# Which engine normalises the attention rows in the first slots, and where the second sum of a weight conversion stands on Pool

## The chip, the cores and the metric

The kernel runs on one core of one Trainium2 chip. The metric is the device time of one execution in microseconds (us). The engines are named as the profile names them: PE (matrix products and transposes), DVE (vector), ACT (activations and most copies), POOL or Pool (GpSimd), SP (which here only issues transfers, DMAs). Each engine runs its own queue of instructions in order and waits on semaphores for the others.

## What is computed

```python
B, H, S, D = 8, 8, 576, 64;  top_k = 32          # q, k, v: (B, H, S, D)
scores = (q @ k.T) / sqrt(D)
kth    = 32nd largest score of each row
scores = where(scores >= kth, scores, -1e9)
attn   = exp(scores - rowmax);  attn = attn / (sum(attn) + 1e-9)
x      = (attn @ v) as (B*S, H*D) = (4608, 512)
out    = gelu_exact(x @ w_in) @ w_out             # w_in (512, 2048), w_out (2048, 512)
```

q, k and v are float32; w_in and w_out arrive as float64 and are converted in the kernel.

## The kernel before

**Items and slots.** The attention is cut into 144 items. An item is 128 rows of scores for a pair of heads side by side (the last 64 rows of four heads are packed into one item), in one tile `s` of 128 partitions x 2 x 576. The loop at L616 makes one pass per item, plus four; I call a pass a slot, n counts them from 0. The order of the work is written out by hand: there is no scheduler, each engine gets its instructions in the order in which the loop emits them. Several items are in work at once. Slot n does, in this order:

- `weights_add` of the weight unit that belongs to slot n (L619; see below), the scores of item n + 2 (L620, PE into PSUM, and ACT copies them to `s`, L280 and L281), the product with v of item n - 3 (L621, PE L443, every second slot, then an ACT copy to `xT`, L448);
- transposes of item n - 2 (L624): first the tails (PE L394, ACT copy L395), then four each of the two halves (PE L412, ACT copies L419). Their PSUM buffers are two, shared with other small products, so the second half waits until ACT has emptied the tails' buffer;
- the softmax of item n - 1 on ACT (L362 masks with the threshold `neg`, L363 is the exponential with the row's sum into `den`), for both halves before the tails' copy up to slot 10, and for one half before and one behind it later (`late`, L622);
- `add_small` of item n - 1 on Pool (L355: `den` + 1e-9);
- `top_k` of item n on DVE (L323 and L326: four rounds of the eight largest for two halves), with `inverse` (L349: 1 / `den` of item n - 1, into `rden`) at its end;
- `threshold` of item n on Pool (L338 and L341: `neg` and `bias`, which the softmax of item n needs in slot n + 1);
- `normalise` of item n - 1 (L375, s times `rden`, one instruction per half): on Pool, on DVE, or one half each, by its second argument (L660);
- `weights_size` of the unit of slot n + 1 on ACT (L174, L176 and, before slot 10, L178), and the loads on SP: `load_weights` of the unit of slot n + 2 (L664, L159), and `v` (L666).

Between these the loop places pieces of the two MLP products (`mlp`, PE L495 and L531, ACT's GELU L506), as soon as there are finished rows of `xT`: the first stands in slot 10.

**The weights.** The two weight matrices come in 16 units of 128 x 1024 numbers. A unit of float64 words is loaded into a staging area, and is turned into float32 by whole-number arithmetic: ACT makes two or three parts from the words (`weights_size`), and Pool adds them up: `weights_add` does the first sum (L193) and the second (L194). Units stand in slots 1 to 15 and 17. From slot START = 10 on (`on_pool`) one of ACT's parts is made by Pool instead (L190). The staging area of a unit is loaded again for the unit two slots later, so that load waits for the second sum.

**Who normalises before.** Where slot n + 1 has a weight unit of START or later, DVE normalises both halves; where it has an earlier one, Pool has the first half and DVE the second; where it has none, Pool has both.

Of the kernel before, what the change touches and what calls it, by code (L numbers as in the profile page):

```python
# [14 lines left out]
def kernel(  # L15
# [97 lines left out]
    def weights_of(u):  # L113

        if u < NWI:
            c, r = u // 2 * WS, u % 2 * 2
            return w_in, r, c, w_in_sb[:, r : r + 2, c : c + WS]
        r = 2 * (u - NWI)
        return w_out, r, 0, w_out_sb[:, r : r + 2, :]
# [6 lines left out]
    words = {}  # L126
# [8 lines left out]
    unit_in = UNIT_IN.get  # L135
# [29 lines left out]
    def parts(u):  # L165

        t, dst = words[u], weights_of(u)[3].bitcast(i32)
        return t[:, :, 0::2], t.bitcast(mybir.dt.int16)[:, :, 2::4], t[:, :, 1::2].bitcast(i32), dst
# [11 lines left out]
    def on_pool(u):  # L180

        return SLOT_OF[u] >= START

    made = set()

    def weights_add(u):
        if u in words:
            w, _, below, d = parts(u)
            if on_pool(u):
                nc.gpsimd.tensor_scalar(  # L190
                    w.bitcast(i32), w.bitcast(u32), 2.0**-13, None, op0=ALU.mult
                )
            nc.gpsimd.tensor_tensor(d, d, below, op=ALU.add)  # L193
            nc.gpsimd.tensor_tensor(d, d, w.bitcast(i32), op=ALU.add)  # L194
        made.add(u)


    items, starts = [], []
# [47 lines left out]
    def row(i, e):  # L246
        return S_of[i][:, e * S : (e + 1) * S]
# [60 lines left out]
    def top_k(i, hooks):  # L308


        stat_of[i] = st = {
            "top": work.tile([P, 2, TOPK], f32, tag="top", name="top"),
            "neg": work.tile([P, 2, 2], f32, tag="neg", name="neg"),
            "bias": work.tile([P, 2], f32, tag="bias", name="bias"),
            "den": work.tile([P, 2], f32, tag="den", name="den"),
            "rden": work.tile([P, 2], f32, tag="rden", name="rden"),
        }
        cur = [row(i, e) for e in range(2)]
        rest = work.tile([P, 2, S], f32, tag="rest", bufs=1, name="rest")
        n_op = 0  # L320
        for r in range(TOPK // 8):
            for e in range(2):
                nc.vector.max(st["top"][:, e, 8 * r : 8 * r + 8], cur[e])  # L323
            if r < TOPK // 8 - 1:
                for e in range(2):
                    nc.vector.match_replace(  # L326
                        rest[:, e], st["top"][:, e, 8 * r : 8 * r + 8], cur[e], LOWEST
                    )
                cur = [rest[:, e] for e in range(2)]
            if r in hooks:  # L330
                hooks.pop(r)()

    def threshold(i):

        if i < 0 or i >= N:
            return
        st = stat_of[i]
        nc.gpsimd.tensor_scalar(  # L338
            st["neg"], st["top"][:, :, 0 :: TOPK - 1], -1.0, None, op0=ALU.mult
        )  # L340
        nc.gpsimd.tensor_tensor(  # L341
            st["bias"], st["neg"][:, :, 0], st["neg"][:, :, 1], op=ALU.subtract
        )

    def inverse(i):
        if i < 0 or i >= N:
            return
        st = stat_of[i]
        nc.vector.reciprocal(st["rden"], st["den"])  # L349

    def add_small(i):
        if i < 0 or i >= N:
            return
        st = stat_of[i]
        nc.gpsimd.tensor_scalar(st["den"], st["den"], 1e-9, None, op0=ALU.add)  # L355

    def softmax(i, e):

        if i < 0 or i >= N:
            return  # L360
        st, s = stat_of[i], row(i, e)
        nc.scalar.activation(s, s, func=AF.Prelu, bias=st["neg"][:, e, 1:2], scale=1.0, alpha=STEEP)  # L362
        nc.scalar.activation(  # L363
            s, s, func=AF.Exp, bias=st["bias"][:, e : e + 1], scale=1.0,
            accum_out=st["den"][:, e : e + 1],
        )

    def normalise(i, on_dve):

        if i < 0 or i >= N:  # L370
            return
        st = stat_of[i]
        for e in range(2):
            s = row(i, e)
            (nc.vector if e >= 2 - on_dve else nc.gpsimd).tensor_scalar(  # L375
                s, s, st["rden"][:, e : e + 1], None, op0=ALU.mult
            )
# [5 lines left out]
    def transposes(i):  # L383

        if i < 0 or i >= N:
            return []
        t, s = items[i][1], S_of.pop(i)

        def tails():
            tp = ps.tile([P, 512], f32, tag="tp", name="tp_t")  # L390
            if t < NM:
                if t % 2 == 0:
                    pt_now[0] = work.tile([P, 2 * NM + 1, 2 * P], f32, tag="pt", name="pt")
                nc.tensor.transpose(tp[:, 0:P], s[:, SM : S + TL], ident)  # L394
                nc.scalar.copy(out=pt_now[0][:, 2 * NM, t % 2 * P : (t % 2 + 1) * P], in_=tp[:, 0:P])  # L395
            else:
                pt_now[0] = ptt
                for r in range(2):
                    nc.tensor.transpose(
                        tp[0:TL, r * P : (r + 1) * P], s[:, r * S + SM : (r + 1) * S], ident  # L400
                    )
                for e in range(2):
                    c = slice(e * TL, (e + 1) * TL)
                    nc.scalar.copy(
                        out=halves(ptt[c, 0, NM, :], e, NJ * P), in_=halves(tp[0:TL, 0 : 2 * P], e, P)
                    )

        def main(e):
            tp = ps.tile([P, 512], f32, tag="tp", name="tp")
            first = e * (S + TL if t < NM else S)  # L410
            for j in range(NM):
                nc.tensor.transpose(  # L412
                    tp[:, j * P : (j + 1) * P], s[:, first + j * P : first + (j + 1) * P], ident
                )
            if t < NM:
                dst = pt_now[0][:, e * NM : (e + 1) * NM, t % 2 * P : (t % 2 + 1) * P]
            else:
                dst = ptt[:, e, 0:NM, :]
            nc.scalar.copy(out=dst, in_=tp.rearrange("p (j n) -> p j n", j=NM))  # L419

        return [tails] + [lambda e=e: main(e) for e in range(2)]
# [137 lines left out]
    def run_gelus():  # L559
        while waiting:  # L560
            gelus(waiting.pop(0))
# [9 lines left out]
    def mlp(n):  # L571
        for _ in range(n):
            if done[0] >= len(pieces) or pieces[done[0]][0] > ready[0] or left[0] == 0:
                return
            pieces[done[0]][1]()
            done[0] += 1
            left[0] -= 1
# [38 lines left out]
    for n in range(ahead):  # L616

        left[0] = 7 if START < n < START + 2 * NP else 8
        weights_add(unit_in(n))  # L619
        scores(n + 2)  # L620
        product = attend(n - 3)  # L621
        late = n > START  # L622
        mlp(1)
        tr = transposes(n - 2)  # L624
        if product and n > START and done[0] < len(pieces) and pieces[done[0]][0] > ready[0]:

            for piece in tr[:1]:
                piece()
            tr, ready[0] = tr[1:], n_tok[0]
        softmax(n - 1, 0)  # L630
        mlp(1)
        if not late:
            softmax(n - 1, 1)
        mlp(1)
        prep = prep_in.pop(n, [])
        if len(prep) > 1 and len(tr) == 3:
            tr, prep = tr[:1] + prep[:1] + tr[1:], prep[1:]
        for piece in tr[:-1]:
            piece()
            ready[0] = n_tok[0]  # L640
            mlp(1)
        ready[0] = n_tok[0]
        if late:
            softmax(n - 1, 1)
        add_small(n - 1)
        for piece in tr[-1:] + prep:
            piece()
            mlp(1)

        run_gelus()  # L650
        mlp(left[0])
        run_gelus()
        if n < N:
            top_k(n, {3: lambda: inverse(n - 1)})
        else:
            inverse(n - 1)
        threshold(n)
        u = unit_in(n + 1)

        normalise(n - 1, 0 if u not in words else 2 if on_pool(u) else 1)  # L660

        weights_size(unit_in(n + 1))
        if n >= FIRST:
            load_weights(n + 2)  # L664
        if n <= NP:
            load("v", n)  # L666
# [38 lines left out]
```

## Time and profile before

| | |
|---|---|
| time, three runs | median 1655.15 us (1654.75 to 1656.08) |
| the profiled execution | 1655.42 us, its span 1653.7 us |
| busy in the span: PE, DVE, ACT, Pool | 1593.8, 1419.6, 1184.1, 650.5 us |
| normalising on Pool (L375) | 266 instructions, 1723 ns each |
| normalising on DVE (L375) | 22 instructions, 520 ns each (median) |
| second sums on Pool (L194) | 16 instructions, about 2.40 us each |
| busy on Pool between 33.0 and 43.3 us (about slot 2) | 7.23 of 10.3 us |
| busy on DVE in the same stretch | 10.27 of 10.3 us |
| first product of the MLP on PE (L495) | starts at 117.94 us |

Times inside an execution count from the start of its span. A row of the timeline gives the start, the duration, the engine, the line, the operation and its tiles; in brackets stands how long the engine had been idle before it and what released it. A row of the waits gives who waited for whom: total us, how often, and the longest. A row of the chain that ended last gives start, duration, engine, tile and line of each step, followed back from the last instruction. The granted clock is PE's, 1.0 at full speed.

### The profile page before, as it was taken

How to read it: one execution, taken by the hardware profiler on the slowest of the kernel's cores; microseconds unless marked ns; L12 is line 12 of the kernel's file. 1: busy time of each engine (PE TensorE's matmuls, PEld its weight loads, DVE VectorE, ACT ScalarE, POOL GpSimd, SP SyncE). 2: the span in 40 equal slices, each digit the busy share in tenths (PEclk: the TensorE clock that was granted, in tenths of full speed). 3: DMA queues.
4: the chain of work that ended last, by engine and by line, in shares of the span. 5: the costliest groups of instructions: out<-in, count | busy, mean ns of one | idle time of the engine just before them, and what ended most of it. 6: DMA issues, size and time to landing. Idle time of an engine off the chain costs nothing.

```text
span 1653.7 us, 25056 instructions
## 1 busy us (share of the span) xinstructions
PE 1593.8 (96%) x8832; PEld 1080.5 (65%) x8832; DVE 1419.6 (86%) x3049; ACT 1184.1 (72%) x2131; POOL 650.5 (39%) x756
## 2 busy tenths in 40 slices
PE   6669999999999999999999999999999999999999
PEld 4346566766666667676666667676666666666665
DVE  7999899989999889998989988998889898999800
ACT  6888777777777777777777777777777777777720
POOL 3677543333333333333333333333333333333300
PEclk7669999999999999999999999999999999999999
DMA  6423210011101111011110111001110001000000
GB/s 165 139 98 102 83 43 1 14 29 29 50 1 28 30 30 28 1 28 36 29 28 1 42 29 43 1 14 28 44 35 1 27 15 34 2 14 4 4 13 13
DMA packets 126621, 56.14 MB, mean 34 GB/s; under 512 B 117760, under 2 KB 117792, under 8 KB 126496
## 3 DMA queue, kind: packets, MB, share of 16 engines
q1 hardware_dynamic: 125376, 54.25, 12.2%
q8 instruction: 70, 1.15, 0.3%
q14 instruction: 55, 0.45, 0.1%
q10 hardware_dynamic: 1056, 0.26, 0.1%
q0 software_dynamic: 64, 0.03, 0.0%
HBM read 45.08 MB, written 9.44 MB: 33 GB/s over the span
## 4 chain that ended last, share of the span: by engine, by line
PE 92%; ACT 6%; DVE 1%; issue 1%; POOL 0%; ACTq 0%; POOLq 0%; DVEq 0%
PE h_ps L495 30%; PE y_ps L531 30%; PE o L443 9%; PE s_ps L276 8%; PE tp L412 8%; PE tp_qk L231 2%; PE t_ps L272 2%; ACT s L363 1%; PE o L454 1%; ACT s L362 1%; PE s_ps L297 1%; PE tp_t L394 1%; ACT s L280 1%; POOL s L375 0%; PE warm L595 0%
## 5 line engine op out<-in xcount | busy, mean ns | idle before, releaser
L323 DVE MAX8 top<-rest 128x8 f32<-128x576 f32 x864 | 608.9, 746 | 0.0
L495 PE MATMUL h_ps<-xT,w_in_sb 128*128 128x256 f32 (+1 forms) x2560 | 554.5, 362 | 3.8 <-ACT g L506 3.8
L531 PE MATMUL y_ps<-w_out_sb,g 128*128 128x512 f32 x1152 | 549.5, 599 | 0.0
L495 PEld LDWEIGHTS h_ps<-xT,w_in_sb 128*128 128x128 f32 x2560 | 429.6, 191 | 66.6 <-issue 19.6
L375 POOL TENSOR_SCALAR s<-s,rden 128x576 f32<-128x576 f32 x266 | 456.0, 1723 | 0.8 <-issue 0.4
L326 DVE MATCH_REPLACE8 rest<-top,rest 128x576 f32<-128x576 f32 x576 | 423.0, 741 | 0.0
L355 POOL TENSOR_SCALAR den<-den 128x2 f32<-128x2 f32 x144 | 32.0, 222 | 835.2 <-ACT s L363 834.4
L531 PEld LDWEIGHTS y_ps<-w_out_sb,g 128*128 128x128 f32 x1152 | 195.1, 190 | 166.8 <-issue 165.0
L280 ACT ACTIVATE s<-s_ps 128x1024 f32<-128x1024 f32 x128 | 131.5, 1027 | 167.3 <-PE s_ps L276 149.1
L363 ACT ACTIVATE s<-s,bias 128x576 f32<-128x576 f32 x288 | 223.3, 776 | 13.3 <-ACT s L362 0.7
L362 ACT ACTIVATE s<-s,neg 128x576 f32<-128x576 f32 x288 | 223.9, 778 | 0.3 <-POOL neg L338 0.2
L419 ACT COPY pt<-tp 128x512 f32<-128x512 f32 x256 | 147.1, 574 | 103.0 <-PE tp L412 103.0
L412 PEld LDWEIGHTS tp<-ident,s 128*128 128x128 f32 x1152 | 145.9, 144 | 111.9 <-issue 59.1
L326 DVE MATCH_REPLACE8 rest<-top,s 128x576 f32<-128x576 f32 x288 | 211.6, 742 | 0.0
L323 DVE MAX8 top<-s 128x8 f32<-128x576 f32 x288 | 201.8, 742 | 3.9 <-ACT s L281 3.9
L412 PE MATMUL tp<-ident,s 128*128 128x128 f32 x1152 | 178.6, 279 | 23.6 <-ACT pt L395 22.0
L443 PE MATMUL o<-pt,raw_v 128*64 128x256 f32 x1280 | 155.5, 390 | 0.0
L276 PE MATMUL s_ps<-qk 64*128 64x256 f32 x1024 | 153.9, 421 | 0.7 <-ACT s L280 0.7
L349 DVE RECIPROCAL rden<-den 128x2 f32<-128x2 f32 x144 | 23.0, 160 | 142.1 <-POOL den L355 141.8
L443 PEld LDWEIGHTS o<-pt,raw_v 128*64 128x64 f32 x1280 | 87.8, 139 | 66.2 <-issue 23.4
L276 PEld LDWEIGHTS s_ps<-qk 64*128 64x128 f32 x1024 | 92.5, 195 | 23.7 <-issue 1.6
L506 ACT ACTIVATE g<-h_ps 128x512 f32<-128x512 f32 x144 | 78.6, 595 | 34.0 <-PE h_ps L495 33.2
(66 smaller groups left out, 1088.3 us busy)
## 6 DMA issues: line engine op xcount, KB each, us to landing
raw_q<-in_q_dram SPq DMA_DIRECT2D x64, 128.0 KB, 2.4
raw_v<-in_v_dram SPq DMA_DIRECT2D x64, 128.0 KB, 2.5
out_dram<-y SPq DMA_DIRECT2D x32, 256.0 KB, 2.1
w_out_sb<-in_moe_w_in_dram SPq DMA_DIRECT2D x16, 511.8 KB, 4.9
raw_k<-in_k_dram SPq DMA_DIRECT2D x62, 128.0 KB, 2.5
w_out_sb<-in_moe_w_out_dram SPq DMA_DIRECT2D x10, 511.8 KB, 3.9
words<-in_moe_w_out_dram SPq DMA_DIRECT2D x6, 511.8 KB, 4.5
raw_q<-in_q_dram SPq DMA_DIRECT2D x64, 16.0 KB, 2.3
```

The costliest lines, as they stand in the source:

```text
L276: nc.tensor.matmul(s_ps[:, e, c * 256 : (c + 1) * 256], lhsT=lhsT[rows, :], rhs=qk[rows, KT + c * 256 : KT + (c + 1) * 256], start=True, s ...
L280: nc.scalar.activation(spread(s, S + TL, SM), s_ps, func=AF.Copy, scale=scale)
L323: nc.vector.max(st["top"][:, e, 8 * r : 8 * r + 8], cur[e])
L326: nc.vector.match_replace(rest[:, e], st["top"][:, e, 8 * r : 8 * r + 8], cur[e], LOWEST)
L362: nc.scalar.activation(s, s, func=AF.Prelu, bias=st["neg"][:, e, 1:2], scale=1.0, alpha=STEEP)
L363: nc.scalar.activation(s, s, func=AF.Exp, bias=st["bias"][:, e : e + 1], scale=1.0, accum_out=st["den"][:, e : e + 1],)
L375: (nc.vector if e >= 2 - on_dve else nc.gpsimd).tensor_scalar(s, s, st["rden"][:, e : e + 1], None, op0=ALU.mult)
L412: nc.tensor.transpose(tp[:, j * P : (j + 1) * P], s[:, first + j * P : first + (j + 1) * P], ident)
L419: nc.scalar.copy(out=dst, in_=tp.rearrange("p (j n) -> p j n", j=NM))
L443: nc.tensor.matmul(o[e * D : (e + 1) * D, 0:n], lhsT=vt[:, j, e, :], rhs=pt[:, e * NM + j if j < NM else 2 * NM, :], start=(j == 0), stop= ...
L495: nc.tensor.matmul(h_tile(u)[:, i, :], lhsT=w_in_sb[:, ko, f * P : (f + 1) * P], rhs=xT[:, ko, c0 : c0 + n], start=(ko == 0), stop=(ko == ...
L531: nc.tensor.matmul(y_of[sub], lhsT=g_of[u][:, i, sub * P : (sub + 1) * P], rhs=w_out_sb[:, f, :], start=(f == 0), stop=(f == FT - 1),)
```

## The change

In the first slots (weight units of slots 2 to 9) DVE normalises nothing any more, Pool does both halves. From START on it is as before. The second sum of each weight unit goes into a function of its own, `weights_end`, which is called behind `add_small`, in all 16 slots that have a unit; the first sum and, from START on, L190 stay at the start of the slot.

```diff
                 nc.gpsimd.tensor_tensor(d, d, below, op=ALU.add)
-            nc.gpsimd.tensor_tensor(d, d, w.bitcast(i32), op=ALU.add)
         made.add(u)
+
+    def weights_end(u):
+        if u in words:
+            w, _, _, d = parts(u)
+            nc.gpsimd.tensor_tensor(d, d, w.bitcast(i32), op=ALU.add)
...
         add_small(n - 1)
+        weights_end(unit_in(n))
         for piece in tr[-1:] + prep:
...
-        normalise(n - 1, 0 if u not in words else 2 if on_pool(u) else 1)
+        normalise(n - 1, 2 if u in words and on_pool(u) else 0)
```

The queues then read, for slot 5 on Pool: before, neg, bias, one L375, first sum, second sum, L355; after, neg, bias, two L375, first sum, L355, second sum. On DVE the instruction between L349 and the next selection is gone in slots 1 to 8. The transfers of a unit wait on SP for the second sum, wherever that stands.

More of the change, by code (lines that the diff above doesn't have):

```diff
@@ L193, in weights_add @@
             nc.gpsimd.tensor_tensor(d, d, below, op=ALU.add)
+        made.add(u)
+    def weights_end(u):
+        if u in words:
+            w, _, _, d = parts(u)
             nc.gpsimd.tensor_tensor(d, d, w.bitcast(i32), op=ALU.add)
-        made.add(u)
     items, starts = [], []
```

## The prediction

> **What bounds the kernel now.** The page's first part has PE busy for 96% of the span, but its forty slices show 6, 6, 6 in tenths for PE at the start: about the first 124 us are not PE's. The diff touches only slots 1 to 17, so I read that stretch. (Slot n is one pass of the loop at L616; DVE starts its selection for slots 1, 2, ... 9 at 22.7, 33.0, ... 105.1 us.) First DVE's timeline at the end of slot 4 (start, duration, engine, line, operation):
>
> ```profile
> 63.19 0.14 DVE L349 RECIPROCAL rden<-den 128x2 f32<-128x2 f32 x1
> 63.36 0.52 DVE L375 TENSOR_SCALAR s<-s,rden 128x576 f32<-128x576 f32 x1
> 63.81 1.41 DVE L323 MAX8 top<-s 128x8 f32<-128x576 f32 x2
> ```
>
> DVE never rests here: in the windows by slot it is busy 10.27 of each 10.3 us, and the waits list has no row for DVE between 20 and 118 us. The multiplication holds up the next selection by 63.81 - 63.36 = 0.45 us. So it looks as if DVE set the pace. Does anyone wait for it? These are all waits of ACT from 20 to 118 us:
>
> ```profile
> ACT pt L419 <- PE tp L412: 4.6, 9, 0.7
> ACT xT L448 <- PE o L443: 4.5, 4, 1.8
> ACT s L280 <- PE s_ps L276: 2.9, 1, 2.9
> ACT s L280 <- DVE rden L349: 0.3, 1, 0.3
> ACT qk L235 <- PE tp_qk L231: 0.3, 1, 0.3
> ```
>
> ACT waits for PE, and once, for 0.3 us, for something put down to DVE (at 114.92; PE's scores for that copy end at 114.83, so I take it for PE's). It never waits for `neg`, which DVE's selection releases. PE does wait for Pool's normalised rows, so I follow that wait in slot 5:
>
> ```profile
> 65.70 0.48 PE L394 MATMUL tp_t<-ident,s 128*128 128x128 f32 x1 [2.05 <-POOL s L375]
> 66.46 1.11 PE L412 MATMUL tp<-ident,s 128*128 128x128 f32 x4 [0.28 <-ACT s L281]
> 69.80 1.12 PE L412 MATMUL tp<-ident,s 128*128 128x128 f32 x4 [2.23 <-ACT pt L395]
> ```
>
> PE waits 2.05 us for Pool, transposes, and waits again, 2.23 us, for ACT to empty a PSUM buffer. ACT does that at 69.50, directly after its two softmaxes (66.31 to 69.50), without having waited. What Pool delays is therefore hidden behind ACT. The chain that ended last says the same: ACT and PE alternate, and no DVE or Pool step stands in it before 198.71 us.
>
> ```profile
> 107.59 0.87 ACT s L363 x2
> 108.46 0.67 ACT s L362
> 109.14 0.02 issue
> 109.16 0.87 ACT s L363 x2
> 110.03 0.16 ACT pt L395
> 110.19 0.04 issue
> 110.23 1.13 PE tp L412 x4
> ```
>
> So DVE, and ACT with PE, are two nearly equal loops of 10.3 us a slot. The second is on the path; DVE runs ahead of it: Pool's `bias` from the previous selection is ready 1.4 us before ACT's softmax starts in slot 2 (33.1 against 34.50), and 2.6 us before in slot 10 (115.6 against 118.19).
>
> **The change, part by part.** *DVE.* In slots 1 to 8 (n + 1 from 2 to 9) one of two multiplications leaves DVE: 8 x 0.45 = 3.6 us, period 10.27 - 0.45 = 9.82. Its selection for slot 9 ends at about 110.9 and not 114.75. At START = 10 the weights are Pool's, and DVE keeps both multiplications as now. There it already waits: in slot 11 it idles 1.17 us until 137.54, for `den`, which ACT's softmax (end 137.2) releases. Now it would come at about 132.6 and wait 4.9 us for the same event. So the 3.6 us are lost at 137.5 unless ACT or PE used them earlier, and no ACT row did. Gain: 0 to 0.3 us, the one doubtful wait; I take 0.1.
>
> *Pool.* Each of these slots gains one L375 at 1.70 us (start to start, 33.12 to 34.82): 8 x 1.70 = 13.6 us. The order becomes neg, bias, two L375, L193, L355, then the second sum (before L194). By starts that is 0.31 + 0.26 + 3.43 + 2.48 + 0.30 + 2.48 = 9.3 us, under 9.82, plus the wait of L355 for ACT. Going through the slots: the wait of L355 for softmax ends at 60.5, 80.3 and 100.5 (slots 4, 6, 8), so the second sum ends at 63.3, 83.1, 103.3, and `neg`, queued behind it, starts there and no longer at DVE's 61.9, 81.5, 101.2. It is still before ACT's use at 66.31, 86.10, 106.74. The two L375 then end at 36.6, 46.4, 67.4, 87.2, 107.3 in slots 2, 3, 5, 7, 9, where they ended at 34.9, 45.1, 65.7, 86.3, 107.0. PE's tail transpose (0.5 us) and its four L412 (1.1 us) move with them; in slot 2 four L231 do. ACT takes the tails at 37.71, 48.46, 69.50, 89.30, 109.93. The tightest is slot 2, 37.1 against 37.71; then the L412 of slot 5, 68.8 against 69.65. Cost 0, covered by ACT's softmaxes. Without that cover it would cost each move: 1.7 + 1.3 + 1.7 + 0.9 + 0.3 = 5.9 us.
>
> *The moved sum, slots 10 to 17.* Here L355 comes late from ACT (137.28, 148.07, 159.81, 172.02, 186.93 in slots 11 to 15), the second sum now starts 0.30 us behind it and takes 2.49, and what is queued behind it on Pool is `neg` and `bias`, for which ACT's next softmax waits. `neg` starts at 140.1, 150.9, 162.6, 174.8, 189.7 instead of 137.6 to 187.2 and takes 0.23; ACT's L362 uses it at 141.92, 154.51, 164.56, 176.09, 191.46. The least slack is about 1.1 us, in slot 14. ACT's L363 needs `bias` 0.9 us later than L362 needs `neg`, and it is ready 0.3 to 0.8 us after it. Cost 0. In slot 15 the two L375 behind them end at 193.63 instead of 191.15, and PE's tail transpose, its work before it ending at 193.93, starts at 193.77: 0 to 0.1 us. In slot 17 `neg` is due at 209.9 either way, DVE's selection and the sum ending together: 0 to 0.1 us.
>
> *DMA on SP.* The load for slot n + 2 waits for the second sum of slot n, because it reuses that staging. It moves from 60.3 to 63.3 (slot 4), 70.5 to 72.6, 80.8 to 83.1, 101.5 to 103.3, 146.6 to 150.9 and, most, 182.8 to 189.7 (slot 15). The second of its two transfers is issued 0.4 us later, and landing takes 3.3 to 7.2 us, median 4.4. ACT's L174 needs them at 71.44, 81.65, 91.24, 112.13, 160.57, 199.54: even at 7.2 us they land at 70.9, 80.2, 90.7, 110.9, 158.5 and 197.3. Behind them in SP's queue stand loads of `v` (issued at 40.6 and 61.1 us behind those of slots 2 and 4) whose first use by PE comes more than 30 us later. Cost 0.
>
> *PE's clock.* It goes to full at 54.8, 75.3, 95.8 and 116.2 and back at 61.6, 82.1, 102.6, all 20.5 us apart, twice six steps of 3.41 us in two slots. The moved transposes fill such a step differently, above all 37.6 to 41.0 us (PE busy in 84% of it, then about 92%). What a flip would do isn't shown; one step at half clock is worth 3.41 / 2 = 1.7 us of PE at most, either way. I take 0, since in that slot the full clock would shorten s_ps (2.08 us) while ACT is busy with weights.
>
> The Trainium skill ("TensorE: Matmul & The Clock Gate", Part 1) states free-running windows of 3413 ns that raise the clock after a busy one; the trace's steps of 3.41 us agree. By that rule a flip depends on where the window lies in a run, and the sum would be the same give or take 1.7 us.
>
> The page "GPSIMD Engine Reference" (introduction) speaks against this change: ordinary elementwise arithmetic is the wrong work for that engine, Vector being roughly twice as fast. Here it is 1723 ns against 520, 3.3 times. By the rule eight multiplications would be an estimated 8.3 us more on Pool, by the rows 13.6; both lie under Pool's idle time, so the end doesn't move by either.
>
> **Sum.** -0.1 + 0.1 = 0.0 us. The profiled execution took 1655.42 us (span 1653.7 and 1.7 around it); the median of three is 1655.15, 0.3 lower. Predicted: **1655.2 us**, with its own range 1653.4 to 1657.0 (the clock's 1.7 us and 0.1).
>
> **Rivals.** *DVE was the bound after all.* For it: no idle time at all in eight slots, and PE at 60%. Against: no wait of ACT for `neg`. If all of it reaches the first h_ps (117.94), the rest follows 3.6 us earlier: 1651.6.
> *The moved sum makes ACT wait for `neg`.* For it: five slots in which Pool gets 2.49 us behind, in a stretch where PE is on the path. Against: slacks of 1.1 to 3.4 us. It decides as soon as ACT reaches L362 in slots 11 to 15 over 1.1 us earlier than today, or L355 comes that much later against it. Fully uncovered it is 5 x 2.49 = 12.4 us, 1667.6; half covered, which I take, 6.2 us: 1661.4.
> *The change doesn't do what it says.* It does: in the order of instructions DVE loses eight multiplications, Pool gains eight, and the second sum stands behind L355 in each of the 16 slots.
>
> **How the numbers follow.** Chances: forecast 0.75, DVE the bound 0.13, the wait for `neg` 0.12. What a measurement of this kernel can tell from no change is about 0.2%, 3.3 us. The forecast's own range lies within that, the rivals lie outside, one on each side. For 8 in 10 I add the faster rival and leave the slower one out: 1651.4 to 1658.0, the upper end for a wait for `neg` in one slot, 2.49 us, on top of the forecast.
>
> **What would show it.** Right: DVE's L375 falls from 22 to 14, Pool's rises from 266 to 274 (busy +13.8 us); the first h_ps stays within 0.5 us of 117.94; DVE's wait for `den` in slot 11 grows from 1.2 to about 4.9 us; PE's wait for Pool's s grows by about 6 us from 11.9 before 120 us, and ACT's softmax in slots 2 to 10 stays in its place. Wrong: an ACT wait for Pool's neg or bias anywhere before 200 us, a weight load that ACT waits for, or an h_ps that starts at 114.

## The result, and the profile after

The changed kernel takes 1660.18 us (median of 6 runs, 1659.04 to 1660.72), the kernel before beside it 1655.09 us (6 runs, 1654.27 to 1656.08): a ratio of 1.003, interval 1.0017 to 1.0042. It is slower by about 5 us, and lies outside the predicted range of 1651.4 to 1658.0. The profiled execution took 1660.2 us.

All line numbers from the second sum on are four or five higher now: the second sum is L199 (it was L194), `neg` and `bias` L342 and L345, the reciprocal L353, `den` L359, the softmax L366 and L367, the normalisation L379, and the first MLP product L499. (`h_ps` is the tile that this product writes; "the first h_ps" is its first instruction.) The page of the changed kernel, its first lines and the row of Pool's normalisations:

```profile
span 1658.4 us, 25046 instructions
## 1 busy us (share of the span) xinstructions
PE 1594.9 (96%) x8832; PEld 1081.7 (65%) x8832; DVE 1422.9 (86%) x3041; ACT 1185.1 (71%) x2131; POOL 663.5 (40%) x764
...
L379 POOL TENSOR_SCALAR s<-s,rden 128x576 f32<-128x576 f32 x274 | 470.1, 1726 | 0.4 <-DVE rden L353 0.4
```

The span is 4.7 us longer and PE is busy only 1.1 us longer, so most of the loss is PE's idle time. Pool has its eight instructions more (274 for 266). DVE has eight fewer and is still busy 3.3 us *longer* (1422.9 for 1419.6); the last section comes back to that. The first places to look are those that the prediction showed. DVE's timeline at the end of slot 4, changed kernel:

```profile
61.09 0.17 DVE L353 RECIPROCAL rden<-den 128x2 f32<-128x2 f32 x1 [0.45 <-POOL den L359]
61.17 1.40 DVE L327 MAX8 top<-s 128x8 f32<-128x576 f32 x2
```

The multiplication between the two is gone, and DVE, early now, waits 0.45 us for `den`. PE's wait in slot 5, changed kernel:

```profile
67.47 0.47 PE L398 MATMUL tp_t<-ident,s 128*128 128x128 f32 x1 [2.98 <-POOL s L379]
67.75 1.06 PE L416 MATMUL tp<-ident,s 128*128 128x128 f32 x4
70.56 1.11 PE L416 MATMUL tp<-ident,s 128*128 128x128 f32 x4 [1.76 <-ACT pt L399]
```

PE waits longer for Pool (2.98 for 2.05 us) and nearly as much less behind it (1.76 for 2.23 for ACT's copy, and the four L416 between them no longer wait 0.28): Pool's delay is swallowed, as predicted. All of ACT's waits from 20 to 118 us, changed kernel:

```profile
ACT pt L423 <- PE tp L416: 5.5, 9, 0.7
ACT xT L452 <- PE o L447: 3.2, 2, 2.2
ACT qk L239 <- PE tp_qk L235: 1.7, 3, 1.1
ACT s L284 <- PE s_ps L280: 0.3, 1, 0.3
```

Their sum is 10.7 us, before it was 12.6, and Pool isn't among them. ACT loses nothing to Pool here. The list of ACT's waits from 118 to 215 us has one row with a releaser that is nowhere in the list of before:

```profile
ACT w_out_sb L174 <- POOL w_out_sb L199: 2.1, 1, 2.1
```

L174 is ACT's first step of the weight conversion (`weights_size`), and what it waits for is the moved second sum. The chain that ended last in the changed kernel passes exactly there (start, duration, engine, tile, line):

```profile
171.58 0.69 ACT s L366
172.28 0.88 ACT s L367 x2
173.24 0.23 POOL den L359
173.54 2.41 POOL w_out_sb L199
175.97 1.27 ACT w_out_sb L174
```

In the part of the chain that the prediction showed, ACT and PE alternated. Here it leaves ACT at the end of the softmax, goes through Pool's small addition and the second sum behind it, and comes back to ACT. (It takes the same way once more, in slot 6, from 81.48 us. There ACT's timeline has no wait where the chain returns to it: L367 at 88.11 stands directly behind L366. Nothing was lost at that place.) Pool's timeline in slot 14, first before, then after:

```profile
166.72 2.41 POOL L194 TENSOR_TENSOR w_out_sb<-w_out_sb 128x1024 int32<-128x1024 int32 x1
172.02 0.22 POOL L355 TENSOR_SCALAR den<-den 128x2 f32<-128x2 f32 x1 [2.89 <-ACT s L363]
172.32 0.23 POOL L338 TENSOR_SCALAR neg<-top 128x4 f32<-128x4 f32 x1
```

```profile
173.24 0.22 POOL L359 TENSOR_SCALAR den<-den 128x2 f32<-128x2 f32 x1 [3.08 <-ACT s L367]
173.54 2.40 POOL L199 TENSOR_TENSOR w_out_sb<-w_out_sb 128x1024 int32<-128x1024 int32 x1
175.90 0.45 POOL L342 TENSOR_SCALAR neg<-top 128x4 f32<-128x4 f32 x1
```

Before, the sum was done at 169.1, and Pool then stood idle 2.89 us for `den`. Now Pool stands idle first and adds afterwards, until 175.94. ACT's L174 in the same slot, before, then after:

```profile
172.56 1.29 ACT L174 ACTIVATE w_out_sb<-words,low 128x1024 int32<-128x1024 int16 x1
```

```profile
175.97 1.26 ACT L174 ACTIVATE w_out_sb<-words,low 128x1024 int32<-128x1024 int16 x1 [2.08 <-POOL w_out_sb L199]
```

Why does a conversion wait for the sum of another unit? The code says it. The unit of slot 14 is staged in rows 12 to 15 of `w_out_sb` itself (`at = FT // 2 + 4 * (i % 2)` in `load_weights`), since those rows hold no weights yet. The unit of slot 15 is staged elsewhere, but its *destination* is rows 12 and 13 of `w_out_sb` (`weights_of`). L174 writes there what the second sum of slot 14 must have read first. In no other slot are the staging rows of one unit the destination of the next.

From there to the end of the span, the profiled pair adds up so. The first h_ps starts at 119.14 for 117.94, 1.2 us later (experiment 3 comes back to that); L174 is 3.4 us later, so 2.2 us are added at the wait; at the `den` of slot 16 it is still 3.4 (202.13 for 198.71); at 217 us a further 1.3 us come, which are the clock's. Sum 4.7.

The clock's part, in windows cut along the clock's own steps. The columns are the window, its length, busy time (and instructions) of PE, PEld, DVE, ACT and Pool, the granted clock, and the DMAs. Before, then after:

```profile
177.70:181.10 3.40, 0.74 (x6) 0.50 (x5) 3.40 (x9) 3.21 (x7) 3.32 (x2) 1.00 0.35 80
181.10:184.50 3.40, 3.40 (x12) 2.76 (x11) 2.05 (x3) 1.11 (x3) 0.19 (x1) 0.50 0.53 112
...
211.80:215.20 3.40, 1.61 (x8) 1.29 (x9) 3.40 (x9) 0.93 (x3) 2.04 (x2) 1.00 0.02 5
```

```profile
179.30:182.70 3.40, 0.66 (x4) 0.42 (x4) 3.40 (x8) 3.30 (x8) 2.84 (x2) 0.98 0.21 48
182.70:186.00 3.30, 2.11 (x6) 1.67 (x7) 3.30 (x8) 1.52 (x3) 0.00 (x0) 0.50 0.57 128
186.00:189.40 3.40, 3.40 (x13) 2.93 (x12) 0.34 (x1) 2.55 (x4) 0.00 (x0) 0.50 0.01 1
213.30:216.70 3.40, 0.97 (x9) 0.25 (x3) 3.40 (x9) 1.34 (x3) 3.27 (x4) 1.00 0.00 0
216.70:220.10 3.40, 2.78 (x8) 2.25 (x9) 3.40 (x8) 2.21 (x4) 0.56 (x1) 0.50 0.02 5
```

A step in which PE was busy 0.66 to 0.97 of 3.4 us is followed by a step at half clock; one with 1.61 is not. Before, one step ran at half clock here, after, three. The eight products at 217 us take 3.17 us for 1.89, which is the 1.3 us above. Before, then after:

```profile
214.03 1.89 PE L495 MATMUL h_ps<-xT,w_in_sb 128*128 128x256 f32 x8
```

```profile
217.53 3.17 PE L499 MATMUL h_ps<-xT,w_in_sb 128*128 128x256 f32 x8
```

### The profile page after: what moved, and what is told of

The parts are those of the page before. It is cut to its first block, busy times and chain, and to the rows that moved or that the text cites. A ratio compares the mean times of both kernels' runs of the same rounds, so it can differ in the third digit from the quotient of the medians.

```text
span 1658.4 us, 25046 instructions
## 1 busy us (share of the span) xinstructions
PE 1594.9 (96%) x8832; PEld 1081.7 (65%) x8832; DVE 1422.9 (86%) x3041; ACT 1185.1 (71%) x2131; POOL 663.5 (40%) x764
## 4 chain that ended last, share of the span: by engine, by line
PE 91%; ACT 6%; POOL 1%; issue 1%; DVE 1%; DMA 1%; SPq 0%; ACTq 0%; POOLq 0%; DVEq 0%
PE h_ps L499 30%; PE y_ps L535 29%; PE o L447 9%; PE s_ps L280 8%; PE tp L416 7%; PE tp_qk L235 2%; PE t_ps L276 2%; ACT s L367 1%; PE o L458 1%; ACT s L366 1%; PE tp_t L398 1%; PE s_ps L301 1%; POOL s L379 1%; ACT s L284 0%; ACT w_out_sb L178 0%
## 5 line engine op out<-in xcount | busy, mean ns | idle before, releaser
L499 PE MATMUL h_ps<-xT,w_in_sb 128*128 128x256 f32 (+1 forms) x2560 | 556.3, 362 | 4.8 <-ACT g L510 4.8
L499 PEld LDWEIGHTS h_ps<-xT,w_in_sb 128*128 128x128 f32 x2560 | 430.7, 192 | 68.3 <-issue 20.6
L379 POOL TENSOR_SCALAR s<-s,rden 128x576 f32<-128x576 f32 x274 | 470.1, 1726 | 0.4 <-DVE rden L353 0.4
L359 POOL TENSOR_SCALAR den<-den 128x2 f32<-128x2 f32 x144 | 32.1, 223 | 855.4 <-ACT s L367 855.1
L367 ACT ACTIVATE s<-s,bias 128x576 f32<-128x576 f32 x288 | 223.3, 776 | 13.2 <-ACT s L366 0.7
L366 ACT ACTIVATE s<-s,neg 128x576 f32<-128x576 f32 x288 | 223.9, 778 | 0.3 <-POOL neg L342 0.2
L416 PEld LDWEIGHTS tp<-ident,s 128*128 128x128 f32 x1152 | 147.0, 145 | 108.0 <-issue 59.3
L416 PE MATMUL tp<-ident,s 128*128 128x128 f32 x1152 | 179.9, 280 | 19.9 <-ACT pt L399 18.5
L353 DVE RECIPROCAL rden<-den 128x2 f32<-128x2 f32 x144 | 23.1, 160 | 145.1 <-POOL den L359 144.8
```

Of the source, the lines that this page charges most:

```text
L367: nc.scalar.activation(s, s, func=AF.Exp, bias=st["bias"][:, e : e + 1], scale=1.0, accum_out=st["den"][:, e : e + 1],)
L416: nc.tensor.transpose(tp[:, j * P : (j + 1) * P], s[:, first + j * P : first + (j + 1) * P], ident)
L499: nc.tensor.matmul(h_tile(u)[:, i, :], lhsT=w_in_sb[:, ko, f * P : (f + 1) * P], rhs=xT[:, ko, c0 : c0 + n], start=(ko == 0), stop=(ko == ...
```

## The experiments

**Theory.** The whole loss comes from one instruction of the 16 moved ones: the second sum of slot 14, for which L174 waits; about 2.1 us directly, the rest through PE's clock behind the longer idle time. **Rival A:** the eight normalisations on Pool cost it. **Rival B:** the moved sums of slots 10 to 17 cost it through `neg`, the prediction's own rival, or through some other slot. **Rival C:** the 1.2 us at the start are the change's. (In the expectations below, theory 1 is the theory, theory 2 is rival A, and theory 3 says that the clock's steps, which fall differently in each execution, made the difference.)

The first four kernels were measured beside the kernel before, which took 1655.82 us there (30 runs).

**1. The normalisations alone.** The second sum stands again directly behind the first:

```diff
         weights_add(unit_in(n))
+        weights_end(unit_in(n))
...
-        weights_end(unit_in(n))
```

> Only the first half of the change: both normalisations on Pool in the first slots, the second sum left directly behind the first. Theory 1 (the moved sum holds ACT: its L174 for the unit of slot 15 writes rows 12 and 13 of w_out_sb, which are also the staging of slot 14's unit, so it waits for that unit's second sum, 2.1 us in the changed kernel): no wait of ACT for a second sum, and the end of before, 1655.1 us, apart from the clock. Theory 2 (the doubled work on Pool costs PE in the first slots, since the first h_ps came at 119.14 instead of 117.94): first h_ps at about 119.1 again, end 1656.3 or above. Theory 3 (steps of PE's clock that fall differently from execution to execution, not the work, made the first h_ps 1.2 us later and gave another 1.3 us at 217 us): first h_ps anywhere from 117 to 119.5, end 1654 to 1657.

Measured: 1656.21 us (11 runs), ratio 1.0004, 0.9995 to 1.0012. The list of waits has no row for L199, and the timeline of ACT has L174 at its old place, 0.33 us behind the end of `den` (173.61):

```profile
173.94 1.27 ACT L174 ACTIVATE w_out_sb<-words,low 128x1024 int32<-128x1024 int16 x1
```

Rival A falls as the cause of the loss. 13.6 us of work more on Pool and 3.6 us less on DVE show nothing at the end, in either direction; a loss of up to 2.0 us would still lie in the interval. The first h_ps came at 119.31, as theory 2 expected (its end, 1656.3 or above, is just missed); experiment 3 says more on that.

**2. The moved sums alone.** `normalise` as before, second sum behind `add_small` in all 16 slots:

```diff
-        normalise(n - 1, 2 if u in words and on_pool(u) else 0)
+        normalise(n - 1, 0 if u not in words else 2 if on_pool(u) else 1)
```

> Only the other half: the second sum behind the small addition in all slots, normalisations as before. Theory 1: ACT waits about 2.1 us for Pool's second sum before L174 at about 174 us, nowhere else; end 1657.3 to 1658.5 us (2.2 us, up to 3.4 with the PE clock that falls in the longer gap behind it). Theory 2: nothing lost, 1655.1. Theory 3: the same 1655.1 give or take 1.5.

Measured: 1659.83 us, ratio 1.0023, 1.0014 to 1.0032. L174 waits 2.07 us for L199, and the first h_ps starts at 117.21, *earlier* than before. So the cost is in the moved sums. The wait is the one expected; the end is above the expected 1657.3 to 1658.5, so the expectation had set the clock's part too low.

**3. The changed kernel, with the sums moved only in the slots before START.**

```diff
         weights_add(unit_in(n))
+        if n >= START:
+            weights_end(unit_in(n))
...
-        weights_end(unit_in(n))
+        if n < START:
+            weights_end(unit_in(n))
```

> The changed kernel, but from slot 10 on the second sum stays directly behind the first, as before the change. Theory 1: ACT's wait before L174 of slot 15's unit is gone, the end 2.2 to 3.4 us below the changed kernel: 1656.8 to 1658.0, or down to 1655 if the rest was the clock. Theory 2: 1.2 us remain over the kernel before: 1656.3. If neither holds: 1660, as the changed kernel.

Measured: 1656.10 us, ratio 1.0002, 0.9993 to 1.0011. No wait for L199. Up to slot 9 this kernel is the changed kernel, and its time is that of before: Rival C falls as the cause of the loss as well.

Whether the change moves the first h_ps at all is less clear. It came at 118.85 to 119.31 us in the three profiled executions with the normalisations on Pool (the changed kernel, experiments 1 and 3), and at 117.21 to 118.04 in the three without (before, experiments 2 and 4). But experiment 7 below, which is the changed kernel up to slot 14, has it at 117.94, as before. In that execution PE's clock rises at the same times as before (55.0, 75.3, 95.8 and 116.2 us), and ACT's softmaxes of slots 1 to 10 start within 0.1 us of their old places. So with the clock's steps in this place the normalisations cost nothing; in another they may cost about 1 us, which the intervals of experiments 1 and 3 neither show nor exclude.

**4. The kernel before, with one instruction moved:** the second sum of slot 14.

```diff
         weights_add(unit_in(n))
+        if n != 14:
+            weights_end(unit_in(n))
...
         add_small(n - 1)
-        weights_end(unit_in(n))
+        if n == 14:
+            weights_end(unit_in(n))
...
-        normalise(n - 1, 2 if u in words and on_pool(u) else 0)
+        normalise(n - 1, 0 if u not in words else 2 if on_pool(u) else 1)
```

(The edit is shown against the changed kernel, as in experiments 1 to 3.)

> The kernel before with one instruction moved: the second sum of slot 14 alone stands behind the small addition. Theory 1: the same wait of about 2.1 us of ACT at 174 us and the same end as with all sums moved, 1657.3 to 1658.5 us. Theory 2 and 3: one moved sum out of 16 is worth nothing, 1655.1.

Measured: 1660.18 us (8 runs, 1659.68 to 1660.62), ratio 1.0026, 1.0016 to 1.0036. That is 4.4 us above the kernel before beside it, about as much as with all sums moved (4.0 us in experiment 2): the whole loss, and again more than the 1657.3 to 1658.5 expected. ACT's wait, in its timeline:

```profile
174.86 1.25 ACT L174 ACTIVATE w_out_sb<-words,low 128x1024 int32<-128x1024 int16 x1 [2.07 <-POOL w_out_sb L199]
```

Its first h_ps is at 118.04, as before, so this execution shows the pure effect: L174 comes 2.3 us late, and the span ends 5.1 us late. The windows between show where the other 2.8 us come from:

```profile
177.70:181.10 3.40, 0.74 (x5) 0.42 (x4) 3.40 (x8) 3.30 (x8) 3.32 (x2) 1.00 0.18 42
181.10:184.50 3.40, 1.75 (x4) 1.41 (x5) 3.40 (x9) 1.98 (x3) 2.41 (x2) 0.51 0.56 127
184.50:188.00 3.50, 3.50 (x14) 2.95 (x12) 0.72 (x2) 2.30 (x3) 0.00 (x0) 0.50 0.82 303
212.00:215.40 3.40, 1.13 (x9) 0.40 (x5) 3.40 (x9) 1.50 (x4) 3.11 (x4) 0.99 0.00 0
215.40:218.80 3.40, 2.62 (x7) 2.18 (x8) 3.40 (x8) 2.05 (x4) 0.72 (x1) 0.50 0.02 5
218.80:222.20 3.40, 3.40 (x11) 2.73 (x11) 3.02 (x7) 2.66 (x6) 0.00 (x0) 0.51 0.01 2
```

Four steps at half clock, for one before, but only the last two cost time. PE starts h_ps 2.0 us later, so the step from 181.1 is only half filled, which doesn't bring the clock back. Yet at the `den` of slot 16 this execution is still only 2.3 us late (200.99 for 198.71), and so are the tail transposes of slot 18 (214.47 for 212.19). Then, at 212 us, a step has 1.13 us of PE work where before it had 1.61, and the clock falls. The eight products behind it take 3.62 us for 1.89, and the four L416 at 222.27 are 5.2 us late (before: 217.06).

This second fall doesn't need the wait. PE's two idle gaps there, 1.64 and 1.41 us, are the same in before, the changed kernel and experiments 1 to 4, to 0.01 us. Experiment 3, without the wait, has the fall too (3.37 us for its eight products), experiment 1 hasn't (1.89), and experiment 2 has it (3.62). It depends on how the gaps lie against the clock's steps, and the wait is one thing that moves them.

Is that really the clock, or something else that the wait shifts? The next four kernels (the kernel before beside the first two: 1655.70 us, 31 runs) put products of the identity matrix, whose results nothing uses, in front of PE's late work, to hold the clock up.

**5 and 6. Filling PE's idle time in slots 15 and 18.** `stall_fill(k)` is k such products; it is called ahead of the first h_ps of slot 15 and ahead of the transposes of slot 18:

```diff
+    slot = [0]
+
+    def stall_fill(k):
+        t = ps.tile([P, 512], f32, tag="tp", name="fill")
+        for _ in range(k):
+            nc.tensor.matmul(t[:, 0:P], lhsT=ident, rhs=ident, start=True, stop=True)
...
             run_gelus()
+            if slot[0] == 15:
+                stall_fill(20)
...
         mlp(1)
+        slot[0] = n
+        if n == 18:
+            stall_fill(12)
         tr = transposes(n - 2)
```

(20 in the changed kernel, 16 in the kernel before.)

> The changed kernel, with idle PE time filled in two places: 20 products of the identity (128x128, result unused) ahead of the h_ps that waits for the GELU in slot 15, and 12 ahead of the tail transposes that wait for Pool in slot 18. They compute nothing that is used. Theory 1 in its present form (of some 4.4 us, 2.1 are ACT's wait itself; the rest is PE at half clock at 183 to 189 and 215 to 222 us, which the longer gap brings on): ACT's wait stays at 2.1 us, the clock stays full in both places, the end is 1657.0 to 1658.2 us. If the clock is not the cause of the rest: 1660, or later by the fillers.

> The kernel before with the same fillers (16 and 12). Theory 1: there the clock falls only at 181 to 184.5 us in the profile shown, worth about 1.2 us (8 h_ps at 1.7 for 1.0 us a group of four), so 1654.3 to 1655.2 us; the difference to the changed kernel with fillers is the bare wait, 2.1 to 2.5 us. If the clock is not the cause: 1655.8, no change.

Measured: the changed kernel with them 1659.31 us, ratio 1.0025, 1.0016 to 1.0035; the kernel before with them 1656.02 us, ratio 1.0, 0.9991 to 1.0009. Both miss what was expected if the clock is the cause (1657.0 to 1658.2 and 1654.3 to 1655.2). The clock was held (no step at half clock from 118.5 on in the changed kernel, nor behind 115 us in the kernel before), but the fillers stood in the way, as PE's timeline of the changed kernel with 20 of them shows:

```profile
181.24 4.73 PE L497 MATMUL fill<-ident 128*128 128x128 f32 x40 [1.12 <-ACT pt L399]
185.81 1.03 PE L510 MATMUL h_ps<-xT,w_in_sb 128*128 128x256 f32 x4
```

One product is two PE instructions, so 20 take 4.73 us, and h_ps starts 10.0 us behind L174, where without them it is 7.9. In the kernel before, 16 took 3.84 us, and h_ps came 9.1 us behind L174 for 8.2. So what the fillers saved by the clock they gave back at least in part, and this pair decides nothing.

**7 and 8. The same with 10 products in slot 15** (12 in slot 18 as above; the kernel before beside them: 1655.49 us, 27 runs).

> The changed kernel with fillers that fit into PE's gaps: 10 products of the identity (each took 0.23 us at full clock in the run with 20, where they held up h_ps by 2.1 us) ahead of the h_ps in slot 15, and 12 ahead of the tail transposes of slot 18, which there delayed nothing. Theory 1 (2.1 us of ACT's wait, the rest PE at half clock behind it): ACT still waits 2.1 us, the clock stays full at 183 to 189 and 215 to 222 us, end 1657.0 to 1658.3. If the clock is not the rest: 1659.5 to 1660.2, as without fillers.

> The kernel before with the same short fillers. Theory 1: what is left between it and the changed kernel with fillers is the bare wait, 2.1 to 2.5 us; itself 1653.7 to 1655.2, since the clock's fall at 181 us (about 1.2 us) goes and no filler delays h_ps. If the clock plays no part: 1655.7.

Measured: changed kernel 1657.26 us (1656.91 to 1657.82), ratio 1.0012, 1.0003 to 1.0021; kernel before 1654.61 us, ratio 0.9994, 0.9985 to 1.0002. In the first of them L174 still waits 2.07 us for L199, while the eight products at 217 us are back at their 1.89 us, by PE's timeline:

```profile
216.28 1.89 PE L510 MATMUL h_ps<-xT,w_in_sb 128*128 128x256 f32 x8
```

With the clock mostly held in both (one step at half clock in the first, 181.1 to 184.4, none in the second behind 118 us), the difference between them is 2.65 us, near the bare wait of 2.07 and as expected. Without fillers it is 4.0 to 5.1 (experiments 2 and 4 and the result). So about half of the loss is the wait, and the rest comes by the clock. By these medians the split holds to about 1 us only, because the ten products run at half clock in the first (3.85 us, and h_ps comes 9.1 us behind L174 for 7.9) and at full in the second (2.50 us, and 8.2 as without them).

The profiled executions divide it better. In experiment 7 the clock's steps lie as in experiment 4, and so does `den` of slot 16 (200.96 and 200.99 us, before 198.71). At the forty products with `ptt` that PE does behind the late part of slot 18 (L458, before L454) they are at 225.45 and 228.40, before at 223.19. From there to the end the kernel before, the changed one and experiments 1 to 4, 7 and 8 all take 1430.4 to 1430.5 us. So in this place of the clock's steps 2.3 us come with the wait and 2.9 with the fall behind 215 us, and with the fillers of slot 18 the second part is gone.

**9 and 10. Fillers in slots 1 to 9.** Would DVE's 3.6 us count, if PE's clock didn't slow the other loop? Fourteen products ahead of the tails' transposes (`transposes` only lists the work, which is emitted further down) and fourteen ahead of the second half, in slots 1 to 9; once in the kernel before, once in the kernel of experiment 3 (which has the normalisations on Pool, and no wait in slot 14). Both ran beside 5 and 6.

```diff
+    def fill(n, k):
+        if 1 <= n < START:
+            for _ in range(k):
+                nc.tensor.matmul(warm[:, 0:P], lhsT=ident, rhs=ident, start=True, stop=True)
...
         tr = transposes(n - 2)
+        fill(n, 14)
...
         add_small(n - 1)
+        fill(n, 14)
         for piece in tr[-1:] + prep:
```

> The kernel before with PE's idle time in slots 1 to 9 filled: 14 products of the identity ahead of the tail transposes and 14 ahead of the second half's transposes; nothing of them is used. It asks whether PE's half clock in the first slots is on the path. If it is: the clock stays full from slot 2 on, ACT's waits for PE up to 118 us (12 us) fall to about 5, until DVE, busy without pause, takes over as the bound: its selection for slot 9 ends at 114.75, so the first h_ps can't come more than 2.6 us earlier than 117.94; end 1653.2 to 1655. If the first slots are bound by ACT alone: 1655.8. If the fillers stand in the way: above 1657.

> Both normalisations on Pool in the first slots, the second sum moved only before slot 10 (so ACT never waits for it), and the same fillers in slots 1 to 9. If PE's clock is on the path in the first slots, and DVE next to it, then DVE's 3.6 us count here and not without the fillers: first h_ps at 112 to 115, end 1650 to 1653 us, 2 to 3 us below the kernel before with fillers. If DVE's work is hidden all the same: as that one. If Pool, with 9.3 us of work a slot, becomes the bound: above it, with waits of PE for Pool's s in every slot.

Measured: 1658.49 us, ratio 1.0018, 1.0009 to 1.0026, and 1657.92 us, ratio 1.0016, 1.0007 to 1.0024. Inconclusive for the question, and the second well above the 1650 to 1653 expected: the clock was up almost throughout, but the fillers delayed the transposes, and ACT's waits for them rose from 4.6 us to 12.6 and 11.2. The first h_ps came at 121.55 and 119.96.

**11 and 12. Shorter fillers in both places.** `fill(n, 9)` ahead of the tails and `fill(n, 3 if product else 8)` ahead of the second half, with the 10 and 12 products of slots 15 and 18; first the kernel of experiment 3, then the kernel before. They ran beside 7 and 8.

> Both normalisations on Pool in the first slots, the second sum moved only before slot 10, short fillers in slots 1 to 9 (9 ahead of the tail transposes, 8 or 3 ahead of the second half's, so that they end before ACT frees the buffer) and the two of slots 15 and 18. With PE at full clock ACT's waits for PE fall from 12 us to about 4 and its slot to about 9.5 us, so DVE's 9.82 us a slot bind: first h_ps at 112 to 114.5, end 1649 to 1652. If the first slots are bound by ACT's own work: 1654. If the fillers still stand in the way: 1656 or more.

> The kernel before with the same fillers in all three places. DVE keeps its 10.27 us a slot: if the clock is on the path in the first slots, the first h_ps comes up to 2.6 us earlier and not more, end 1651.5 to 1653.5, and the same fillers with Pool normalising are 1 to 3 us faster: only there the 3.6 us taken off DVE count. If both come out the same, DVE is hidden even then.

Measured: 1650.54 us (5 runs, 1648.72 to 1650.65), ratio 0.9968, 0.9955 to 0.998; and 1651.98 us (11 runs, 1650.22 to 1653.47), ratio 0.9978, 0.9969 to 0.9987. Both are faster than the kernel before, and the first, 5 us below it, is the fastest of the study. Its waits of ACT from 20 to 112 us, then those of the second from 20 to 116:

```profile
ACT pt L423 <- PE tp L416: 5.0, 9, 1.6
ACT qk L239 <- PE tp_qk L235: 0.9, 1, 0.9
```

```profile
ACT pt L419 <- PE tp L412: 6.0, 9, 2.4
ACT s L280 <- PE s_ps L276: 2.7, 1, 2.7
ACT s L362 <- POOL neg L338: 0.2, 1, 0.2
ACT xT L448 <- PE o L443: 0.2, 1, 0.2
```

With PE's clock up, the kernel before shows the first wait of ACT for `neg` (0.2 us): now DVE's loop is just the slower one, and taking the multiplications from it has something to give. The difference, 1.4 us, is less than the 3.6 of DVE's work, and the two sets of runs overlap by 0.4 us; that the gain exists at all is likely but not settled. The first h_ps came at 112.32 against 116.37, 4.0 us earlier, of which 2.7 are left at the end of these two executions (spans of 1647.0 and 1649.7 us); where the rest goes wasn't followed. The fillers' own gain, 1651.98 against 1655.49, is settled.

## Why the prediction was wrong

Its steps, in its own order:

- *DVE: the 3.6 us are lost.* Right. Experiment 1 is 1.0004. Its DVE waits 4.84 us for `den` in slot 11; predicted 4.9. So close a number is partly luck: DVE comes only 2.3 us earlier than before (134.07 for 136.37), since it has already waited 1.27 us for `den` in slots 9 and 10, and `den` comes 1.4 us later. In the changed kernel itself that wait is only 2.86 us, for a reason that the prediction didn't have (last section).
- *Pool: 13.6 us hidden behind ACT's softmaxes.* Right for the waits, and in detail: `neg` of slots 4, 6 and 8 starts at 63.51, 84.16 and 103.28 (predicted 63.3, 83.1, 103.3), PE's wait for Pool's s rises from 11.9 to 17.5 us (predicted about 18), and ACT has no row for Pool before 118 us. But the first h_ps, which was to stay within 0.5 us of 117.94, came at 119.14; experiment 3 has what is known of that.
- *The moved sum, slots 10 to 17: cost 0.* **This step failed.** It counted what stands behind the second sum on Pool, that is `neg` and `bias`, and the transfer that reuses the staging area. On all of these it was right: no ACT wait for `neg` or `bias` appeared. But it didn't ask who reads or overwrites the tile that the moved instruction itself uses. L174 of slot 15's unit does; its slack was 172.56 - 169.13 = 3.4 us before, and the sum moved by 173.54 - 166.72 = 6.8 us, of which about 1.2 are the later start of this execution. 3.4 - 5.6 = -2.2, and 2.08 was measured. It could have been worked out beforehand from rows that the prediction had: `den` at 172.02, 0.30 to the sum, 2.41 for it, so 174.73 against 172.56, a wait of 2.17 us in slot 14. Experiment 4 shows that it is the whole loss. The prediction's closing list does name "a weight load that ACT waits for" as what would prove it wrong, but only with the transfers in mind.
- *DMA on SP: cost 0.* Right: no ACT row for a DMA between 20 and 215 us.
- *PE's clock: at most 1.7 us either way, taken as 0.* Too small, and in the wrong place. For the first 118 us, where the prediction looked, nothing of it is measured at the end (experiments 1 and 3). But the price was set for one step, and behind slot 14, where it didn't look, the clock cost more: two half-clock steps behind 215 us in experiment 4, some 2.9 us of its 5.1.
- *The rival on the slower side* had the right object, the moved sum, and the right engine, ACT, but the wrong wait: `neg` in five slots, 12.4 us uncovered, in place of the staging area in one, 2.1 us and the clock.

The Trainium skill ("TensorE: Matmul & The Clock Gate", Part 1) has the clock follow windows that run free of the kernel's start. The runs agree: the fall behind 180 us comes at 181.1 in the kernel before and at 182.7 in the changed one, which is no whole number of 3.41-us steps apart. The same page's closing table ("Why this matters for your kernels") warns of idle gaps over about 3 us. Here that is too lenient: the two idle gaps of PE that reach into the changed kernel's step from 213.3 are 1.64 and 1.41 us long, it is busy 0.97 of 3.4 us, and the clock falls all the same.

What stays open: how the 4 to 5 us divide between wait and clock on average over executions, to better than 1 us; whether the normalisations cost anything when the clock's steps lie otherwise; and whether the changed kernel would be free of loss with the unit of slot 14 staged in memory of its own; that wasn't tried.

## What to carry to other kernels

When an instruction is moved back, ask three things of it: what is queued behind it on its engine, who reads what it writes, and who *overwrites what it reads*. The last is invisible in a trace of before, as long as it is early enough: look for buffers that borrow the space of others, and compare the new end of the moved instruction with the start of the borrower. And where an engine's clock follows its own load, a wait ahead of it can cost more than its length, by the half-clock steps that follow and that nothing covers: here 2.1 us became 4 to 5.

## What was not expected of the hardware

**DVE's multiplication beside Pool's sum.** DVE lost eight instructions and was busy 3.3 us longer. The two normalisations that it keeps from slot 9 on, taken together, last 0.95 us in the kernel before. In slot 9 of the changed kernel, by DVE's timeline:

```profile
111.59 2.91 DVE L379 TENSOR_SCALAR s<-s,rden 128x576 f32<-128x576 f32 x2
```

and Pool's timeline beside it:

```profile
111.06 0.22 POOL L359 TENSOR_SCALAR den<-den 128x2 f32<-128x2 f32 x1 [1.49 <-ACT s L367]
111.36 2.39 POOL L199 TENSOR_TENSOR w_out_sb<-w_out_sb 128x1024 int32<-128x1024 int32 x1
```

`den` releases both: Pool starts its sum 0.23 us before DVE its multiplication, and the multiplication isn't done until the sum is (113.75, and then some 0.7 us more). It happens where the two stand side by side, by 1.96, 0.95, 1.98, 0.02, 0.98 and 1.43 us in slots 9 to 14, 7.3 us in all, twice what the change took from DVE. In experiment 1, where the sum stands early, all are 0.95 us again. The Trainium skill ("SBUF — State Buffer", "Who interferes with whom") says it: a tensor_scalar of DVE in its two-port mode and a Pool instruction lock each other out for a whole instruction, and who starts first wins. That this multiplication runs in that mode no row shows; the rows show that it waits out the sum. It cost nothing that can be seen here, since DVE waits for `den` later on (4.27 us in slot 15): experiment 4, with the 2.91 us in slot 14 alone, ends at the same 1660.18 us as the changed kernel, and experiment 3, with them in slot 9 alone, is at 1.0002. Had DVE been the bound, this would have been the larger part of the bill.

**The clock's return.** After a fall, a step with PE busy 1.75 or 2.11 of 3.4 us didn't bring the full clock back, nor one with 2.62; one with 2.78 did. In the prediction's step at 37.6 us, 84% (about 2.9 us) did not, so the edge isn't sharp in these records. Full steps brought it back in every window shown. So a late start inside a step can mean two steps at half clock and not one.
